# Later releases for the second and third weights load in the start-up of a linear-attention and MLP kernel

## The chip, the cores and the metric

The kernel runs on one core of a Trainium2 chip. The metric is the time of one execution on the device, in microseconds (us). An execution's span, as the profiler records it, is a little shorter than that time.

## The reference

Two blocks follow one another. The first is a linear attention with a decaying state (RWKV6): 4 batches, 8 heads, 768 tokens, 48 channels per head. The second takes its output as rows of 384 numbers and applies a small MLP with 2048 hidden channels, whose activation is h - tanh(h).

```python
for t in range(S):
    kt, vt, rt, wt = (k[:, :, t], v[:, :, t], r[:, :, t], w[:, :, t])
    cur = np.einsum('bhd,bhe->bhde', u[None] * kt, vt)
    y[:, :, t] = np.einsum('bhd,bhde->bhe', rt, state + cur)
    state = wt[:, :, :, None] * state + np.einsum('bhd,bhe->bhde', kt, vt)
...
h = x @ w_in
g = h - np.tanh(h)
return (g @ w_out).astype(np.float32)
```

All is float32 to the outside, and the weights are passed as they are (no arithmetic on the host).

## The kernel before, in words

The 3072 tokens are worked off in eight blocks of 384 tokens (4 batches times 2 halves of the sequence). Inside a block, the attention is computed in six chunks of 64 tokens, for four pairs of heads. For each block the result is laid down transposed, as three tiles `xT0` to `xT2` (xT in the profile) of 128 channels by 384 tokens, which feed the MLP. The MLP takes 16 steps f per block: `first` (L883) multiplies xT by one tile of `w_in` and gives h, ScalarE and VectorE form g, and `Second.add` (L962) or other products add g times `w_out`. While the MLP of one block runs, the attention of the next is prepared between its steps. The instructions of TensorE (PE), VectorE (DVE), ScalarE (ACT) and SyncE (SP) run in the order in which the program lists them: each engine has one queue, and an instruction that waits holds up all behind it on that engine. SyncE's instructions are the starts of transfers.

The first block has no MLP to hide behind. Its attention is computed in `boot` (from L1140), in two halves of two head pairs each, called h1 and h2. The order there is written out by hand. For each half:

- `behind`, `before`, `times_behind`, `times_before` form running products of the decay on VectorE;
- `own` and `earlier` compute the scores (L494): `own` those of a token with itself (the diagonal mask), `earlier` those with the tokens before it in its chunk, the off-diagonal ones;
- `turn_1` (L517) and `turn_2` (L523) transpose the keys;
- `update_half` (L616) makes, with 24 small matmuls on TensorE, what each chunk adds to the state;
- `states_half` (L631) carries the state from chunk to chunk on VectorE;
- `result` multiplies scores with v (L698) and states with the decayed r (L679), and `result_out` (L741) copies the outcome out of PSUM into xT, on ScalarE and VectorE.

Head pairs 0 to 2 go to their own xT tile; each tile has holes of 16 rows, which pair 3, kept in the tile `late`, fills by six copies of 24 KB from on-chip memory to on-chip memory (`fill_holes`, L789), three begun by SyncE and three by GpSimd.

The weights arrive as raw tiles (`raw`, 768 KB each) by transfers that SyncE begins (`load_weights`, L251, called by `more_weights`). Sixteen loads bring all weights, and five buffers hold the raw tiles. The first and second load bring the first four steps' tiles of `w_in`; the third brings the first two steps' tiles of `w_out`; the fourth brings `w_in` again. Each raw tile is then converted (`convert`): three steps on ScalarE (L264), of which one writes `w_sb` and two write `up`, and a joining step on VectorE (L268). In `boot`, `first_a`, `second_a`, `third_a` are the ScalarE steps for the first three loads, and `first_b`, `second_b`, `third_b` the VectorE steps. In ScalarE's order `second_a` comes before the last `result_out` of the block, and `third_a` after it.

When a load of weights may start is fixed by `begin_behind(ins, load)`: the load waits until the instruction `ins` is done. Before the change, the second load follows the last matmul of the first half's `update_half`, the third the last matmul of the second half's `own` scores, and the fourth the last matmul of the second half's `earlier` scores (`scored`). The first load waits for nothing, and behind the fourth come the next block's `w` and more weights.

Of the kernel before, what the change touches and what calls it, by code (L numbers as in the profile page):

```python
# [50 lines left out]
B, H, S, D = 4, 8, 768, 48  # L51
# [4 lines left out]
NCH = NB // L  # L56
# [70 lines left out]
def kernel(  # L127
# [12 lines left out]
    nc = tc.nc  # L140
# [29 lines left out]
    start = const.tile([P, UP * NCH * LP], F32, name="start", tag="start")  # L170
# [77 lines left out]
    def load_weights(n, queue):  # L248
        raw = conv.tile([P, 2 * DM, 2], I32, name="raw", tag="raw")
        src = weights[UNITS[n]].bitcast(I32).rearrange("p (n two) -> p n two", two=2)  # L250
        return *UNITS[n], raw, queue.dma_start(out=raw, in_=src)  # L251

    def convert(part, j, raw, _, tiles=1):

        lo, hi = raw[:, :, 0], raw[:, :, 1]
        a = w_sb[:, part, 2 * j:2 * j + 2].rearrange("p f c -> p (f c)").bitcast(I32)
        up = conv.tile([P, 2 * DM], I32, name="up", tag="up", bufs=4)
        low, high = (up.bitcast(t).rearrange("p (n two) -> p n two", two=2)[:, :, i]  # L260
                     for i, t in enumerate((U16, F16)))

        def scaled(to, of, scale, bias=0.0):
            return lambda: nc.scalar.activation(out=to, in_=of, func=AF.Copy, scale=scale, bias=bias)  # L264

        return [scaled(a.bitcast(F32), hi.bitcast(F32), HIGH_SCALE), scaled(high, hi.bitcast(F32), SIGN_SCALE),
                scaled(low, lo.bitcast(U32), *LOW)], [
                lambda of=slice(i * 2 * DM // tiles, (i + 1) * 2 * DM // tiles): nc.vector.scalar_tensor_tensor(  # L268
                    out=a[:, of], in0=a[:, of], scalar=3, in1=up[:, of], op0=ALU.logical_shift_left,
                    op1=ALU.bitwise_or) for i in range(tiles)]  # L270
# [43 lines left out]
    def begin_behind(ins, then):  # L314
        tc.add_manual_dep(then.ins, ins.ins.name, mybir.DependencyInfo(
            mybir.DependencyClass.Sync, mybir.DependencyReason.DATA))
# [3 lines left out]
    class Block:  # L320
# [186 lines left out]
        def own(self, ps, p0, **fill):  # L507
            return self.masked(ps, "k", "r", masks["diagonal"], p0, **fill)

        def earlier(self, ps, p0, **fill):  # L510
            return self.masked(ps, "post", "pre", masks["above"], p0, **fill)
# [90 lines left out]
        def update_half(self, pair, p0):  # L602

            self.by_column = [t[:, 0:D * NCH].rearrange("d (e c) -> d e c", c=NCH) for t in pair]
            for x in range(UP):
                if x:
                    nc.tensor.drain().then_inc(fence, 1)
                    fences.append(None)
                    nc.tensor.wait_ge(fence, len(fences))
                for c in range(0, NCH, 2):  # L610
                    for h in range(2):
                        for par in range(2):
                            p = (x + par) % UP
                            toks = slice(64 * par, 64 * par + 64)
                            e0 = (p0 + p) * D2 + h * D
                            self.done = nc.tensor.matmul(self.by_column[p][64 * h:64 * h + 64, :, (c + par + 1) % NCH],  # L616
                                             lhsT=self.ks[toks, p0 + p, c // 2, 64 * h:64 * h + 64],
                                             rhs=self.v[toks, c // 2, e0:e0 + D], start=True, stop=True)

        def totals_by_column(self, p0):  # L620

# [259 lines left out]
    def first(xT, f, hp, apart=0):  # L881
        for kc in reversed(range(KC)):
            nc.tensor.matmul(hp, lhsT=w_in_sb[:, f, kc, :], rhs=xT[kc],  # L883
                             start=(kc == KC - 1), stop=(kc == 0))
            for _ in range(apart):
                nc.tensor.nop(nofuse=True, hint="apart")
        h = dense.tile([P, NB], F32, name="h", tag="h")
        return h, nc.scalar.activation(out=h, in_=hp, func=AF.Copy, scale=1.0 / UPSCALE)  # L888
# [228 lines left out]
    def more_weights(queue):  # L1117
        raws.append(load_weights(more_weights.n, queue))
        more_weights.n += 1
        return raws[-1][-1]  # L1120
# [3 lines left out]
    def run(ops):  # L1124
        for op in ops:
            op()
# [13 lines left out]
    def boot(ps, pair, blk, later):  # L1140
        h1, h2 = HALVES
        blk.tiles["w"] = states0
        for name, p0, n in (("w", h1 + 1, 1), ("w", h1, 1), ("k", h1, UP), ("r", h1, UP), ("w", h2, UP)):
            blk.load(name, p0, n)
        blk.load_v()
        blk.load("k", h2, UP)
        blk.load("r", h2, UP)
        more_weights(nc.sync)

        both = (h1, h1 + 1), (h2, h2 + 1)  # L1150
        blk.behind(h1 + 1, 1)
        blk.behind(h1, 1)
        blk.take_whole(h1, UP)
        blk.totals_by_column(h1)
        nc.scalar.copy(out=later_ident, in_=ident)
        blk.before(h1, UP)
        blk.times_behind(h1, UP)
        blk.times_u(h1, UP)
        own = blk.own(ps, h1, spare=94, ahead=5, late=6)
        blk.turn_1(ps, h1)  # L1160
        blk.times_before(h1, UP)
        earlier = blk.earlier(ps, h1)
        blk.behind(h2, UP)
        blk.take_whole(h2, UP)
        first_a, first_b = convert(*raws.pop(0), tiles=2)
        own()
        blk.turn_2(h1)
        blk.totals_by_column(h2)
        blk.update_half(pair, h1)
        begin_behind(blk.done, more_weights(nc.sync))  # L1170
        blk.times_behind(h2, UP)
        blk.times_u(h2, UP)
        blk.turn_1(ps, h2)
        blk.turn_2(h2)
        earlier()
        blk.results(ps)
        blk.result("from_scores", both[0])
        blk.in_turn(both[0])
        run(blk.states_half(h1))
        blk.result("from_states", both[0], True, apart=True)  # L1180
        blk.before(h2, UP)
        blk.update_half(pair, h2)
        blk.times_before(h2, UP)
        own = blk.own(ps, h2)
        own_scored = blk.done
        run(first_a[:1])
        blk.result_out((3,), [nc.scalar.copy] * 2)
        blk.result_out((2,))
        earlier = blk.earlier(ps, h2, ahead=1)
        scored = blk.done  # L1190
        onwards = blk.states_half(h2)
        own()
        run(first_a[1:])
        needed = 2 * KC - 2
        blk.fill_holes([nc.sync, nc.gpsimd], range(needed, 2 * KC))
        begin_behind(own_scored, more_weights(nc.sync))
        blk.fill_holes([nc.sync, nc.gpsimd], range(needed))
        begin_behind(scored, more_weights(nc.sync))
        later.load("w")
        second_a, second_b = convert(*raws.pop(0))  # L1200
        third_a, third_b = convert(*raws.pop(0))
        run(second_a)
        more_weights(nc.sync)
        blk.results(ps)
        blk.yp.reverse()
        blk.result("from_states", both[1], apart=True)
        blk.in_turn(both[1])
        earlier(1, 1)
        earlier(0, 1)
        for p in reversed(both[1]):  # L1210
            blk.result("from_scores", (p,), True)
        later.load("k")
        more_weights(nc.sync)
        run(onwards)
        run(first_b[:1])
        for p in reversed(both[1]):
            blk.result_out((p,), [nc.scalar.copy, nc.vector.tensor_copy])
        run(first_b[1:])
        run(third_a[:2])
        run(second_b)  # L1220
        blk.held(0, NPAIR)
        return [(third_a[2], third_b)]
# [6 lines left out]
    with tc.tile_pool(name="ps_boot", bufs=1, space=PSUM) as ps_boot:  # L1229
        pieces = boot(Turns([scratch(ps_boot)] + ps_a.both), [hp] + acc, blocks[0], blocks[1])  # L1230
# [30 lines left out]
    for i, blk in enumerate(blocks):  # L1261
# [9 lines left out]
        for f in range(NF):  # L1271
# [5 lines left out]
            h, made = first(here, f, to[:, 0:NB], SPACED[i][f > 12 + (i < 2)])  # L1277
# [190 lines left out]
```

## Time and profile before

| what | value |
|---|---|
| time, median of 3 runs | 544.36 us |
| lowest and highest | 544.14 and 544.81 us |
| the profiled execution's own time | 543.88 us |
| its span | 542.2 us |
| TensorE busy | 534.0 us (98%) |
| VectorE busy | 459.3 us (85%) |
| ScalarE busy | 404.2 us (75%) |
| transferred | 56.34 MB, of which the 16 weights loads are 768 KB each |

All times in a profile are counted from the start of the span. A timeline row gives start, duration, engine, line, operation, tile written and tiles read, and how many instructions were merged; in brackets stand the time that the engine was idle before it, and what ended that wait. SPq and POOLq are the instructions by which SyncE and GpSimd begin a transfer. PEld is TensorE's loading of weights into its array, which overlaps with its matmuls.

### The profile page before, as it was taken

The page shows a single profiled execution, that of the slowest core. Times are in us where ns is not written, and L with a number is a line of the kernel's source. Part 1 is how long each engine was busy: PE and PEld are TensorE (multiplying, and loading weights), DVE is VectorE, ACT ScalarE, POOL GpSimd, SP SyncE. Part 2 cuts the span into 40 slices and gives each one's busy share as a digit, 9 for nine tenths or more (in the row PEclk, how much of TensorE's full clock was granted, in tenths as well). Part 3 has the DMA queues.
Part 4 walks back from the last instruction along what each step waited for, and adds up shares of the span by engine and source line. Part 5 has one row for each costly group of instructions (what it writes and reads, how often), then busy time and mean ns, then how long its engine had stood idle before and what let it go on. Part 6 is the DMA issues. An engine that isn't in the chain of part 4 may idle for free.

```text
span 542.2 us, 14874 instructions
## 1 busy us (share of the span) xinstructions
PE 534.0 (98%) x5682; PEld 403.4 (74%) x5682; DVE 459.3 (85%) x943; ACT 404.2 (75%) x814; POOL 7.0 (1%) x51
## 2 busy tenths in 40 slices
PE   8999999999999999999999999999999999999996
PEld 5756665678787777877887787877788788777874
DVE  7999999999989989798997989879797997557563
ACT  4999996897668886688767886688766885766561
POOL 1100000000000000000000000000000000000000
PEclk9999999999999999999999999999999999999999
DMA  7799642342311642154122622135321510100101
GB/s 276 242 403 348 219 119 71 122 112 81 106 48 46 162 118 57 44 148 119 61 56 87 132 92 70 50 102 145 90 84 45 118 31 3 56 1 0 45 1 47
DMA packets 53048, 56.34 MB, mean 104 GB/s; under 512 B 21488, under 2 KB 50928, under 8 KB 52976
## 3 DMA queue, kind: packets, MB, share of 16 engines
q1 hardware_dynamic: 52592, 55.18, 33.5%
q8 instruction: 48, 0.79, 0.6%
q14 instruction: 24, 0.20, 0.1%
q10 hardware_dynamic: 288, 0.10, 0.1%
q0 software_dynamic: 96, 0.07, 0.1%
HBM read 44.73 MB, written 4.72 MB: 91 GB/s over the span
## 4 chain that ended last, share of the span: by engine, by line
PE 95%; DVE 2%; DMA 1%; issue 0%; PEld 0%; SPq 0%; PEldq 0%; DVEq 0%
PE hp L883 44%; PE acc L1011 27%; PE att L1011 7%; PE acc L962 5%; PE att L769 4%; PE att L494 2%; PE acc L989 2%; PE att L575 1%; PE att L883 1%; DMA r<-in_rT 1%; PE acc L883 1%; DVE scores L502 1%; DVE post L429 0%; PE att L989 0%; PEld att L679 0%
## 5 line engine op out<-in xcount | busy, mean ns | idle before, releaser
L883 PE MATMUL hp<-xT,w_sb 128*128 128x384 f32 x738 | 259.2, 487 | 0.5 <-DVE w_sb L268 0.5
L883 PEld LDWEIGHTS hp<-xT,w_sb 128*128 128x128 f32 x738 | 131.9, 190 | 69.7 <-issue 0.6
L1011 PE MATMUL acc<-forms,g 128*128 128x128 f32 x954 | 133.2, 276 | 0.0
L888 ACT ACTIVATE h<-hp 128x384 f32<-128x384 f32 x123 | 60.4, 491 | 97.2 <-PE hp L883 97.1
L1011 PEld LDWEIGHTS acc<-forms,g 128*128 128x128 f32 x954 | 122.0, 192 | 10.3
L891 DVE SCALAR_TENSOR_TENSOR h<-h,s 128x384 f32<-128x384 f32 x128 | 70.6, 552 | 51.6 <-ACT s L906 51.5
L932 DVE TENSOR_TENSOR g<-g 128x256 f32<-128x256 f32 x265 | 103.4, 420 | 7.3 <-PE acc L1011 6.5
L907 ACT ACTIVATE qa<-s,shift 128x384 f32<-128x384 f32 x113 | 69.5, 615 | 3.7
L909 ACT ACTIVATE junk<-s,shift 128x384 bf16<-128x384 f32 x113 | 67.7, 599 | 0.0
L891 DVE SCALAR_TENSOR_TENSOR g<-qa,h 128x384 f32<-128x384 f32 x112 | 61.7, 551 | 1.6 <-ACT qa L917 0.2
L906 ACT ACTIVATE s<-h 128x384 f32<-128x384 f32 x113 | 59.1, 523 | 3.5
L1011 PEld LDWEIGHTS acc<-w_sb,g 128*128 128x128 f32 x318 | 46.7, 191 | 9.7 <-ACT sums L979 0.3
L1011 PE MATMUL acc<-w_sb,g 128*128 128x128 f32 x318 | 53.0, 276 | 0.0
L1011 PE MATMUL att<-w_sb,g 128*128 128x128 f32 x212 | 35.5, 275 | 0.0
L1011 PEld LDWEIGHTS att<-w_sb,g 128*128 128x128 f32 x212 | 31.1, 192 | 5.3
L1046 DVE TENSOR_TENSOR sums<-sums 128x256 f32<-128x256 f32 x84 | 32.9, 407 | 1.7 <-ACT sums L1023 1.4
L962 PE MATMUL acc<-w_sb,sums 128*128 128x384 f32 x96 | 33.7, 487 | 0.0
L264 ACT ACTIVATE up<-raw 128x768 f16<-128x768 f32 (+1 forms) x32 | 33.1, 1074 | 0.0
L962 PEld LDWEIGHTS acc<-w_sb,sums 128*128 128x128 f32 x96 | 18.0, 190 | 12.3 <-DVE sums L891 0.3
L417 DVE TENSOR_TENSOR_SCAN pre<-w,start 128x780 f32<-128x780 f32 x14 | 25.0, 1783 | 0.8
L429 DVE TENSOR_TENSOR_SCAN post<-w,seed 128x780 f32<-128x780 f32 x14 | 24.9, 1776 | 0.0
L909 ACT ACTIVATION_READ_ACCUMULATOR junk<-s,shift 128x1 f32 x113 | 21.1, 186 | 0.0
(119 smaller groups left out, 530.5 us busy)
## 6 DMA issues: line engine op xcount, KB each, us to landing
raw<-in_weights SPq DMA_DIRECT2D x16, 768.0 KB, 7.0
w<-in_wT SPq DMA_DIRECT2D x7, 780.0 KB, 4.5
k<-in_kT SPq DMA_DIRECT2D x7, 768.0 KB, 4.6
r<-in_rT SPq DMA_DIRECT2D x7, 768.0 KB, 4.5
v_sb<-in_v SPq DMA_DIRECT2D x8, 576.0 KB, 3.9
k<-in_tokens SPq DMA_DIRECT2D x7, 576.0 KB, 5.0
r<-in_tokens SPq DMA_DIRECT2D x7, 576.0 KB, 4.8
out_y<-sums SPq DMA_DIRECT2D x18, 128.0 KB, 1.8
```

The lines of the kernel that those rows point to most:

```text
L264: return lambda: nc.scalar.activation(out=to, in_=of, func=AF.Copy, scale=scale, bias=bias)
L417: return nc.vector.tensor_tensor_scan(out=self.tile("pre")[:, cols], data0=self.tile("w")[:, cols], data1=start[:, 0:n * NCH * LP], initia ...
L883: nc.tensor.matmul(hp, lhsT=w_in_sb[:, f, kc, :], rhs=xT[kc], start=(kc == KC - 1), stop=(kc == 0))
L888: return h, nc.scalar.activation(out=h, in_=hp, func=AF.Copy, scale=1.0 / UPSCALE)
L891: return lambda: nc.vector.scalar_tensor_tensor(out=out, in0=in0, scalar=scalar, in1=in1, op0=op0, op1=ALU.mult)
L906: nc.scalar.activation(out=s, in_=h, func=AF.Square)
L907: nc.scalar.activation(out=qa, in_=s, func=AF.Square, bias=shift[:, 4:5])
L909: nc.scalar.activation(out=junk[:, 0:NB], in_=s, func=AF.Relu, bias=shift[:, 5:6], accum_out=excess[:, at:at + 1])
L932: return lambda: nc.vector.tensor_tensor(out=G[:, to:to + 2], in0=two(G, g_at(q, a0), g_at(q, a1)), in1=two(G, g_at(q, b0), g_at(q, b1)), ...
L962: nc.tensor.matmul(acc, lhsT=g[:, j * P:(j + 1) * P], rhs=w_out_sb[:, f, :], start=(f == self.first), stop=(f == NF - 1))
L1011: nc.tensor.matmul(to, lhsT=G[:, g_at(q, a), :], rhs=rhs, start=start, stop=stop, skip_group_check=True)
L1046: ops.append(lambda op=op, at=at: nc.vector.tensor_tensor(out=at[0], in0=at[1], in1=at[2], op=OPS[op]))
```

## The change

`update_half` now returns its first matmul. The second load of raw weights waits for the first matmul of the second half's `update_half`, not for the last one of the first half's. The third load waits for `scored`, the last off-diagonal score of the second half, not for the last diagonal score, and SyncE begins it after all its copies of `fill_holes`, where it stood between the first and the other two. The fourth load is released by `scored` as before.

```diff
         def update_half(self, pair, p0):
...
+            first = None
...
-                            self.done = nc.tensor.matmul(self.by_column[p][64 * h:64 * h + 64, :, (c + par + 1) % NCH],
-                                             lhsT=self.ks[toks, p0 + p, c // 2, 64 * h:64 * h + 64],
-                                             rhs=self.v[toks, c // 2, e0:e0 + D], start=True, stop=True)
+                            made = nc.tensor.matmul(self.by_column[p][64 * h:64 * h + 64, :, (c + par + 1) % NCH],
+                                                    lhsT=self.ks[toks, p0 + p, c // 2, 64 * h:64 * h + 64],
+                                                    rhs=self.v[toks, c // 2, e0:e0 + D], start=True, stop=True)
+                            first = first or made
+            return first
...
         blk.update_half(pair, h1)
-        begin_behind(blk.done, more_weights(nc.sync))
         blk.times_behind(h2, UP)
...
-        blk.update_half(pair, h2)
+        begin_behind(blk.update_half(pair, h2), more_weights(nc.sync))
         blk.times_before(h2, UP)
         own = blk.own(ps, h2)
-        own_scored = blk.done
...
         blk.fill_holes([nc.sync, nc.gpsimd], range(needed, 2 * KC))
-        begin_behind(own_scored, more_weights(nc.sync))
         blk.fill_holes([nc.sync, nc.gpsimd], range(needed))
+        begin_behind(scored, more_weights(nc.sync))
         begin_behind(scored, more_weights(nc.sync))
```

## The prediction

> **What bounds the kernel now.** I read the page first, then the sums over long windows, then the timelines of the first 30 us engine by engine, and last the transfers' times from issue to landing.
>
> ```profile
> span 542.2 us, 14874 instructions
> PE 534.0 (98%) x5682; PEld 403.4 (74%) x5682; DVE 459.3 (85%) x943; ACT 404.2 (75%) x814; POOL 7.0 (1%) x51
> L883 PE MATMUL hp<-xT,w_sb 128*128 128x384 f32 x738 | 259.2, 487 | 0.5 <-DVE w_sb L268 0.5
> ```
>
> TensorE is busy for 534.0 of 542.2 us, so nearly all the time is matmuls that this change leaves alone. In the first layer's largest group it idled 0.5 us in all, waiting for VectorE to put a weight tile together. The next view gives busy time by engine (PE, PEld, DVE, ACT, POOL) in two windows.
>
> ```profile
> 29.00:51.00 22.00, 22.00 (x135) 13.46 (x137) 21.28 (x38) 21.90 (x31) 0.00 (x0) 1.00 1.01 391
> 53.00:540.00 487.00, 484.36 (x4920) 370.49 (x4918) 411.90 (x860) 359.15 (x751) 2.37 (x27) 1.00 0.29 81
> ```
>
> From 29 to 51 us, while weights are still being converted, VectorE (21.28 of 22.00) and ScalarE (21.90) are full beside TensorE. After 53 us only TensorE is (484.36 of 487). So a delay that VectorE or ScalarE has at 29 us cannot be caught up by 51 us, and whatever reaches TensorE at 52 us stays to the end. The 0.5 us wait of the page is exactly there:
>
> ```profile
> 52.04 2.17 PE L883 MATMUL hp<-xT,w_sb 128*128 128x384 f32 x6 [0.46 <-DVE w_sb L268]
> ```
>
> The question is therefore what the moved loads do to ScalarE and VectorE before 29 us. The timelines there, starts and durations in us, of TensorE:
>
> ```profile
> 13.14 0.22 PE L616 MATMUL hp<-v_sb,ks 64*64 64x48 f32 x1
> 16.39 0.25 PE L616 MATMUL acc<-v_sb,ks 64*64 64x48 f32 x1
> 19.93 0.22 PE L494 MATMUL att<-pre,post 48*64 48x64 f32 x1
> ```
>
> These are the last update matmul of the first half, the first one of the second half and the last off-diagonal score: the old release of the second load, its new one, and the new release of the third. The issuing queues, SyncE's and GpSimd's:
>
> ```profile
> 13.44 0.34 SPq L251 DMA_DIRECT2D raw<-in_weights  x1
> 17.70 0.64 SPq L789 DMA_DIRECT2D xT<-late  x1
> 18.52 0.43 SPq L251 DMA_DIRECT2D raw<-in_weights  x1
> 19.00 1.15 SPq L789 DMA_DIRECT2D xT<-late  x2
> 20.25 0.53 SPq L251 DMA_DIRECT2D raw<-in_weights  x1
> 16.97 1.58 POOL L789 DMA_DIRECT2D xT<-late  x3 [1.53 <-ACT late L741]
> ```
>
> The three rows of raw are the second, third and fourth load. The second leaves at 13.44, 0.08 us after its matmul ends (13.14 + 0.22). The six small copies that fill the holes of xT stand around the third load. And ScalarE:
>
> ```profile
> 19.44 0.92 ACT L264 ACTIVATE w_sb<-raw 128x768 f32<-128x768 f32 x1
> 20.23 2.02 ACT L264 ACTIVATE up<-raw 128x768 f16<-128x768 f32 x2
> 22.83 0.96 ACT L741 COPY xT<-att 48x384 f32<-48x384 f32 x2 [0.58 <-PE att L698]
> 23.83 0.91 ACT L264 ACTIVATE w_sb<-raw 128x768 f32<-128x768 f32 x1
> 24.63 1.06 ACT L264 ACTIVATE up<-raw 128x768 f16<-128x768 f32 x1
> 25.87 0.49 ACT L888 ACTIVATE h<-acc 128x384 f32<-128x384 f32 x1 [0.17 <-PE acc L883]
> ```
>
> The three steps at 19.44 and 20.23 read the second load. Behind them, in the same queue, stand the copies that finish xT, then the third load's conversion, then the first h. The only idle times are 0.58 and 0.17 us.
>
> **The change, part by part.** No arithmetic is added or removed. Transfers start later and change places on SyncE. How long they take, from five issues of the same 768 KB weights load (asked for at 13.44, 18.52, 50.51, 54.84 and 58.64; last column is us from issue to landing):
>
> ```profile
> raw<-in_weights SPq DMA_DIRECT2D x1, 768.0 KB, 4.3
> raw<-in_weights SPq DMA_DIRECT2D x1, 768.0 KB, 5.3
> raw<-in_weights SPq DMA_DIRECT2D x1, 768.0 KB, 4.2
> raw<-in_weights SPq DMA_DIRECT2D x1, 768.0 KB, 4.1
> raw<-in_weights SPq DMA_DIRECT2D x1, 768.0 KB, 4.5
> ```
>
> *The second load.* Today it lands at 13.44 + 4.3 = 17.74, 1.7 us before ScalarE reads it at 19.44. Its new release ends at 16.39 + 0.25 = 16.64; with the same 0.08 us it is issued at 16.72, 3.28 us later. That exceeds the cover of 1.7 us, so ScalarE must wait. For how long hangs on the transfer. Nothing shows it at 16.72, so it is bounded by 4.1 us (alone) and 5.3 us (the load at 18.52, which shares its time with the hole copies). The new slot lies beside GpSimd's three copies, issued from 16.97, and ahead of SyncE's, so neither row is plainly nearer; I take 4.8 us, between the undisturbed 4.3 and the 5.3. It lands at 21.52. The three conversion steps take from 19.44 to 20.23 + 2.02 = 22.25, that is 2.81 us, and so end at 24.33; with the 0.04 us that usually lie between steps the xT copies start at 24.37 instead of 22.83. The 0.58 us that ScalarE idled there is used up: they are 1.54 us late.
>
> The Trainium skill (DMA: Bandwidth & Descriptors, section "Anatomy of one DMA") fits a DMA of the software path at 2.0 us and its bytes at 436 GB/s; for 786,432 bytes that is an estimate of 3.8 us, and by it the load would land at 20.52 and the end move by 0.4 us, which could not be measured. All five rows here are above it, at 4.1 to 5.3 us, so the rows decide.
>
> *What waits behind it.* VectorE makes the other halves of these copies, and TensorE's weight loads for the first h wait for those and for the holes:
>
> ```profile
> 23.34 1.05 DVE L741 COPY xT<-att 48x384 f32<-48x384 f32 x2 [0.28 <-ACT xT L741]
> 23.18 0.30 PEld L883 LDWEIGHTS acc<-xT,w_sb 128*128 128x128 f32 x2
> 24.11 0.30 PEld L883 LDWEIGHTS acc<-xT,w_sb 128*128 128x128 f32 x2 [0.63 <-DVE xT L741]
> 24.92 0.30 PEld L883 LDWEIGHTS acc<-xT,w_sb 128*128 128x128 f32 x2 [0.51 <-DVE xT L741]
> ```
>
> *The hole copies.* Here the change gives something. SyncE's copy of 17.70, ahead of the third load, and its two of 19.00 and about 19.6, behind it, landed after
>
> ```profile
> xT<-late SPq DMA_DIRECT2D x1, 24.0 KB, 2.0
> xT<-late SPq DMA_DIRECT2D x1, 24.0 KB, 5.0
> xT<-late SPq DMA_DIRECT2D x1, 24.0 KB, 5.2
> ```
>
> so at 24.0 and 24.8, while VectorE's two copies were done by 23.34 + 1.05 = 24.39. The weight load at 24.92 really waited for the last hole, not for VectorE. With the third load behind them these two leave at about 18.3 and 18.9, behind only the second load, and land near 21.5: no wait is left on them. Without them the last weight load could go about 0.32 us earlier (0.65 us of matmuls after one at 23.95). But the xT copies are 1.54 us late, so it goes at 24.60 + 1.54 = 26.14, 1.2 us later than now, and its result comes 0.9 us after that, near 27.05.
>
> *The third and fourth loads.* The last off-diagonal score ends at 20.15, SyncE is free by then, and the third load leaves at about 20.25, 1.73 us later; the fourth, now with the same release, 0.5 us later. At 4.3 to 5.3 us the third lands at 24.55 to 25.55. ScalarE, late anyway, wants it at 23.83 + 1.54 = 25.37: covered within 0.2 us. If ScalarE were on time, this load would be the next to be late, by 0.7 to 1.7 us.
>
> *The sum.* ScalarE's third conversion starts at 25.37, its next step at 26.17 ends at 27.23, and the first h at 27.25 instead of 25.87: 1.38 us, the 1.54 less the 0.17 us of idle time there. VectorE is tied to this:
>
> ```profile
> 26.39 0.56 DVE L914 CUSTOM_DVE_ANT_0 s<-h 128x384 f32<-128x384 f32 x1 [0.46 <-ACT h L888]
> 27.35 0.96 DVE L268 SCALAR_TENSOR_TENSOR w_sb<-w_sb,up 128x768 int32<-128x768 int32 x1 [0.40 <-ACT up L264]
> 28.99 0.56 DVE L891 SCALAR_TENSOR_TENSOR sums<-qa,h 128x384 f32<-128x384 f32 x1 [0.21 <-ACT qa L917]
> 50.96 1.80 DVE L268 SCALAR_TENSOR_TENSOR w_sb<-w_sb,up 128x768 int32<-128x768 int32 x2
> ```
>
> All its idle time before 29 us ends with ScalarE; from 28.99 to the tile that TensorE awaits at 52.04 it has none to give back. So 1.38 us arrive at 52.04, and stay: span 543.6, profiled execution 543.88 + 1.38 = 545.3. The median of the three runs, 544.36, lies 0.48 above that execution; on it the forecast is 545.7.
>
> **The rivals.** *A short transfer.* Everything happens as above, but the load takes 4.1 to 4.3 us, as three of the five rows did. The end moves by 0.7 to 0.9 us: about 545.2. For it: most rows; against it: the hole copies beside it.
>
> *A late chain.* Not only the second load but also the stream behind the third is late, and later conversions wait again. The sixth load, issued at 22.38, landed 12.5 us later, at 34.88, and ScalarE took it at once:
>
> ```profile
> raw<-in_weights SPq DMA_DIRECT2D x1, 768.0 KB, 12.5
> 34.91 0.91 ACT L264 ACTIVATE w_sb<-raw 128x768 f32<-128x768 f32 x1
> ```
>
> Pushed back by the third load's full 1.73 us it lands at 36.61, and ScalarE wants it at 34.91 + 1.38 = 36.29: 0.3 us more, and with a second load of 5.3 us (another 0.5) about 546.5. Against it: the stream no longer has the holes in it and may run faster.
>
> *Not slower: the holes decide.* If the second load landed by 19.98 (22.83 less 0.04 less 2.81), ScalarE's 0.58 us would hide it, and the earlier holes would be what is left: h at about 25.72, 0.15 us sooner, 544.2. It needs a transfer within 3.26 us; no row is below 4.1.
>
> **How the numbers follow.** A measurement of this kernel can tell about 0.2% (1.09 us) from no change; the forecast passes that if the transfer takes over about 4.5 us. Chances: forecast 0.55, short transfer 0.24, late chain 0.09, holes decide 0.08, and 0.04 for a gain that no row shows. Slower by over 0.2%: 0.55 + 0.09 = 0.64; within: 0.24 + 0.08 = 0.32; faster 0.04. The bounds of the transfer alone, 4.1 to 5.3 us, give 545.0 to 546.3; the range reaches to 544.7 and 546.6 to take in half of what lies outside. Cases of slower hold most of the chance.
>
> **What would show it.** In the changed kernel's profile: the second load issued near 16.7 and landing near 21.5; ScalarE idle for about 2 us before the conversion step now at 19.44, its releaser the DMA; no 0.58 us idle before the xT copies; the first h near 27.2; VectorE's step now at 50.96 and TensorE's at 52.04 later by the same amount, about 1.4 us, and nothing lost after. The forecast is wrong if that load lands before 20, if ScalarE's delay is gone by 51 us, or if the page shows new idle time of TensorE after 53 us.

## The result and the profile after

The changed kernel takes 549.5 us (median of six runs, 548.51 to 550.57), the kernel before, run beside it, 544.25 us (six runs, 543.87 to 544.81). The ratio is 1.0096 with a 95% interval of 1.0084 to 1.0108: slower by 1.0%, or 5.25 us. The prediction said slower by 1.38 us, with a range up to 546.6. The direction was right and the size was not. The profiled execution took 548.51 us, 4.63 more than the one of before; it is the fastest of the six.

The head of the page after, and the same group of matmuls as before:

```profile
span 546.8 us, 14873 instructions
PE 535.4 (98%) x5682; PEld 404.3 (74%) x5682; DVE 459.3 (84%) x943; ACT 403.7 (74%) x814; POOL 6.9 (1%) x51
L886 PE MATMUL hp<-xT,w_sb 128*128 128x384 f32 x738 | 259.2, 487 | 0.3 <-DVE w_sb L268 0.3
```

The work is the same; TensorE is busy for 1.4 us more (535.4 against 534.0) and idle for the rest of the 4.6 us. (Below `update_half`, line numbers are 3 higher in the changed kernel: L883 is now L886, L888 is L891, L741 is L744.) Now the start-up, first SyncE's queue and the load's time to landing:

```profile
17.34 0.34 SPq L251 DMA_DIRECT2D raw<-in_weights  x1
18.18 2.04 SPq L792 DMA_DIRECT2D xT<-late  x3
20.59 0.81 SPq L251 DMA_DIRECT2D raw<-in_weights  x2
```
```profile
raw<-in_weights SPq DMA_DIRECT2D x1, 768.0 KB, 6.5
```

The second load leaves at 17.34 and lands 6.5 us later, at 23.88. The trace has 16 completion events for each such load. Fifteen of this one came by 21.80, 4.5 us after the issue, and only the last at 23.88. ScalarE, in the timeline:

```profile
23.90 0.89 ACT L264 ACTIVATE w_sb<-raw 128x768 f32<-128x768 f32 x1 [3.84 <-DMA raw<-in_weights]
24.69 1.95 ACT L264 ACTIVATE up<-raw 128x768 f16<-128x768 f32 x2
26.51 0.81 ACT L744 COPY xT<-att 48x384 f32<-48x384 f32 x2
29.31 0.49 ACT L891 ACTIVATE h<-acc 128x384 f32<-128x384 f32 x1 [0.24 <-PE acc L886]
...
32.83 0.49 ACT L891 ACTIVATE h<-acc 128x384 f32<-128x384 f32 x1 [1.33 <-PE acc L886]
```

It waits 3.84 us for the load, the first h starts at 29.31 instead of 25.87 (3.44 us late), and the second h later still: 32.83, where the kernel before had

```profile
27.97 0.49 ACT L888 ACTIVATE h<-acc 128x384 f32<-128x384 f32 x1
```

so 4.86 us late. The bracket of the second row names its cause, a wait for TensorE. TensorE's clock shows why (columns: window and its length; busy time of PE, PEld, DVE, ACT, POOL; granted clock; share of the DMA engines; GB/s):

```profile
25.50:28.92 3.42, 1.31 (x4) 0.86 (x5) 1.90 (x4) 3.42 (x6) 0.00 (x0) 1.00 1.03 392
28.92:32.33 3.41, 3.41 (x7) 1.72 (x6) 2.65 (x6) 2.35 (x4) 0.00 (x0) 0.50 1.05 393
32.33:53.00 20.67, 20.67 (x74) 12.67 (x73) 18.59 (x34) 20.17 (x29) 0.00 (x0) 1.00 0.91 333
58.00:545.00 487.00, 484.22 (x4920) 370.43 (x4918) 411.79 (x860) 358.62 (x750) 2.35 (x27) 1.00 0.29 81
```

TensorE, without xT, is busy for only 1.31 of the 3.42 us to 28.92; for the next 3.41 us it is granted half its clock, just when it makes the first two h. From 32.33 on it is full again. The hand-over that was at 50.96 and 52.04 comes at

```profile
55.83 1.80 DVE L268 SCALAR_TENSOR_TENSOR w_sb<-w_sb,up 128x768 int32<-128x768 int32 x2
```
```profile
56.91 2.17 PE L886 MATMUL hp<-xT,w_sb 128*128 128x384 f32 x6 [0.30 <-DVE w_sb L268]
```

both 4.87 us late, as the second h was, and the span is 4.6 us longer. After that nothing is lost: TensorE is busy for 484.22 us in the 487 us from 58, against 484.36 in the 487 us from 53 before.

So there are two losses in this execution where the prediction had one: the second load takes 6.5 us, not 4.8, and TensorE's wait is followed by one window at half its clock.

### The profile page after: what moved, and what is told of

Read it like the earlier page. It is cut to its first block, busy times and chain, and to the rows that moved or that the text cites. A ratio compares the mean times of both kernels' runs of the same rounds, so it can differ in the third digit from the quotient of the medians.

```text
span 546.8 us, 14873 instructions
## 1 busy us (share of the span) xinstructions
PE 535.4 (98%) x5682; PEld 404.3 (74%) x5682; DVE 459.3 (84%) x943; ACT 403.7 (74%) x814; POOL 6.9 (1%) x51
## 4 chain that ended last, share of the span: by engine, by line
PE 91%; DVE 3%; ACT 3%; DMA 2%; issue 1%; SPq 0%; PEldq 0%; PEld 0%; DVEq 0%
PE hp L886 43%; PE acc L1014 26%; PE att L1014 6%; PE acc L965 4%; PE att L772 4%; PE att L494 2%; PE acc L992 2%; ACT up L264 1%; PE att L575 1%; DMA raw<-in_weights 1%; PE acc L886 1%; DMA r<-in_rT 1%; DVE post L443 1%; DVE pre L417 0%; DVE w_sb L268 0%
## 5 line engine op out<-in xcount | busy, mean ns | idle before, releaser
L886 PE MATMUL hp<-xT,w_sb 128*128 128x384 f32 x738 | 259.2, 487 | 0.3 <-DVE w_sb L268 0.3
L886 PEld LDWEIGHTS hp<-xT,w_sb 128*128 128x128 f32 x738 | 132.0, 191 | 69.7 <-issue 0.4
L891 ACT ACTIVATE h<-hp 128x384 f32<-128x384 f32 x123 | 60.3, 490 | 97.5 <-PE hp L886 97.4
```

## The experiments

Fourteen runs were made, thirteen of other kernels and one of the changed kernel again, each beside the kernel before on the same chip. Diffs marked "to before" or "to after" are against that kernel. Letters in the quoted expectations are those of the theories when each was written; the text here names them in words.

**The second load's release alone** (to before, with `update_half` returning its first matmul):

```diff
         blk.update_half(pair, h1)
-        begin_behind(blk.done, more_weights(nc.sync))
...
-        blk.update_half(pair, h2)
+        begin_behind(blk.update_half(pair, h2), more_weights(nc.sync))
```

> Only the second load is moved; the third and fourth stay as before the change. Theory A (the loss is the second load's lateness: ScalarE's wait, and the half clock that TensorE is given after its idle time): about the whole loss, 548 to 551 us, with ScalarE waiting 2.5 to 4 us for the load and one stretch of 3.4 us at half clock. Theory B (the third load, late and behind the hole copies, holds a part of 1 us or more): clearly less than the whole, below 548 us.

**The third load's release and place alone** (to before):

```diff
-        begin_behind(own_scored, more_weights(nc.sync))
         blk.fill_holes([nc.sync, nc.gpsimd], range(needed))
         begin_behind(scored, more_weights(nc.sync))
+        begin_behind(scored, more_weights(nc.sync))
```

> Only the third load is moved (released by the last off-diagonal score, after all hole copies); the second stays as before. Theory A: ScalarE is then on time and wants the third load at 23.8 us, while it lands between 24.6 and 25.6: 0.7 to 1.7 us later on ScalarE, 545.0 to 546.0. Theory B: at least as much, with more waits at the fifth and sixth load: over 546. Holes landing earlier can give 0.15 us back at most.

The first took 548.25 us (547.17 to 550.39; ratio 1.0080, 1.0058 to 1.0102), the second 545.4 us (544.24 to 547.7; 1.0020, 1.0008 to 1.0032). ScalarE in the first, then in the second:

```profile
23.32 0.90 ACT L264 ACTIVATE w_sb<-raw 128x768 f32<-128x768 f32 x1 [3.23 <-DMA raw<-in_weights]
```
```profile
25.22 0.93 ACT L264 ACTIVATE w_sb<-raw 128x768 f32<-128x768 f32 x1 [0.88 <-DMA raw<-in_weights]
```

Most of the loss is the second load's; in this first run's profile TensorE had half its clock too, from 26.97 to 30.38 us. The third load, moved alone, makes ScalarE wait 0.88 us, inside the 0.7 to 1.7 us that the prediction gave for a ScalarE that is on time; with the second load late as well, that wait is hidden. In this second profile the second load, in its old place, took 5.6 us (15 of its completion events came by 17.74, the last at 19.08), without harm inside its cover. So the new place is not all that makes a load long.

**Half clock taken away** (to after; `busy` adds eight matmuls whose result nobody reads, while TensorE waits for xT):

```diff
         run(onwards)
+        busy(pair[1], 8)
         run(first_b[:1])
```

> The changed kernel with eight matmuls of 128x512 on the identity (about 0.4 us each, results unused) on TensorE between the last scores and the first matmul of the MLP, so that it isn't idle while it waits for xT. If the half clock is a cost of its own (1.7 us: 3.4 us at half speed), the time falls by 1 to 1.7 us against the changed kernel, to about 548, and the granted clock is 1.0 throughout. If the clock only costs time in which TensorE would have waited for ScalarE anyway, the time stays at 549 to 550.

It took 546.14 us (545.73 to 549.67; 1.0049, 1.0026 to 1.0072), below the 548 that was expected. In its profile the load took 5.5 us, and the window that was at half clock is

```profile
28.92:32.33 3.41, 3.41 (x12) 1.98 (x11) 2.79 (x6) 3.41 (x6) 0.00 (x0) 1.00 1.03 390
```

at full clock; its two h start at 28.04 and 30.14, 2.1 us apart as before (25.87 and 27.97), not 3.5. The runs form two groups: six at 545.73 to 546.3 us, with a mean clock of 0.998 or 0.999, and two at 549.65 and 549.67, with 0.993 and 0.995. Half clock is a loss of its own, 1.4 us between the two h of the changed kernel. What remains without it is the late load, here 1.7 us (546.14 less 544.46 of before beside it) with a transfer that was 1.0 us shorter than in the changed kernel's profile.

**The second load released between the two places** (to before: by the last matmul of the first half's scores times v):

```diff
         blk.update_half(pair, h1)
-        begin_behind(blk.done, more_weights(nc.sync))
...
         blk.result("from_scores", both[0])
+        begin_behind(blk.done, more_weights(nc.sync))
```

> The kernel before with the second load released by the last matmul of the first half's scores times v, which ends near 15.2 us: half way between 13.4 and 16.7. If a transfer at this place takes 4.3 us it lands at 19.6, inside ScalarE's 0.6 us of slack: 544.3, no loss. If a load here takes over 6 us, as the changed kernel's did, it lands near 21.7 and costs about 1.6 us without a change of clock: 546.

545.64 us (544.79 to 546.57; 1.0020, 1.0010 to 1.0031). The load, issued at 15.29, took 4.4 us, and ScalarE did not wait for it. Yet the kernel is slower, through something the prediction does not have:

```profile
21.53 0.50 PE L494 MATMUL att<-pre,post 48*64 48x64 f32 x18 [1.88 <-issue]
```

TensorE stops for 1.88 us in the middle of its scores, and the releaser is "issue": nothing that the profile shows. From 22.37 to 25.79 us, behind this stop, TensorE has half its clock. The changed kernel was then run and profiled **a second time, unchanged**, beside three of the kernels below:

> The changed kernel once more, beside the variants below: 548 to 551 us, with the second load landing 5.5 to 6.5 us after its issue, and one or two stretches of 3.4 us at half clock (mean granted clock 0.993 to 0.997). A load of 4.3 to 4.8 us here would say that the first profile caught a rare one.

549.69 us (547.33 to 550.15; 1.0077, 1.0055 to 1.0099). This time the load was issued at 16.78 and took 6.4 us, and the same stop is there, longer: 4.0 us in the waits, 4.18 us before this weight load. TensorE's clock is halved for two windows, from 20.83 to 27.66 us. The last off-diagonal score comes late through the stop, and so the third load, which it releases, leaves at 24.51 instead of 20.59.

```profile
PE att L494 <- issue: 4.0, 1, 4.0
```
```profile
23.57 0.61 PEld L494 LDWEIGHTS att<-pre,post 48*64 48x64 f32 x18 [4.18 <-issue]
```

What the stop is, the DMA view by windows suggests (queue, kind: packets, MB, share of 16 engines). Of the changed kernel's second profile, from 17 to 20.9 us and from 20.9 to 22.3 us:

```profile
q1 hardware_dynamic: 213, 0.84, 64.2%
q0 software_dynamic: 87, 0.07, 5.2%
```
```profile
q8 instruction: 1, 0.02, 5.4%
...
```

and of before, from 14.8 to 17.3 us, and from 17.3 to 18.3 us:

```profile
q1 hardware_dynamic: 130, 0.72, 74.3%
```
```profile
q0 software_dynamic: 13, 0.02, 8.8%
q8 instruction: 1, 0.02, 6.0%
...
```

q8 carries instructions, 16 KB in one packet. The trace's records of single packets and of completion events give the times (last column: when 15 of the load's 16 events were there, and the last):

```
kernel                   fetches of 16 KB begin at     data of the second load             events: 15, last
before                   13.8, 17.3, 22.7              14.4 to 17.4                        17.66, 17.70
changed, first profile   13.8, 17.6, 21.5              18.3 to 21.2 (120 of 128 rows)      21.80, 23.88
changed, second profile  13.8, 20.95, 24.7             17.8 to 20.96                       21.53, 23.21
released at 15.29        13.9, 19.35, 22.7             16.3 to 19.1                        19.66, 19.70
kept busy                14.0, 17.6, 22.0              18.2 to 21.6                        22.35, 22.67
third load alone         14.0, 17.6, 21.3              14.5 to 18.7                        17.74, 19.08
```

In the kernel before, the load just fits between two fetches. Its last row ends (17.35) when the fetch begins (17.34), so this fetch may have been held a little already, without a stop. Where the load meets the fetch that otherwise comes at 17.3, more than one thing is seen. In the changed kernel's first profile the fetch is first, and the load's last event comes 2.1 us after the other 15. In the second profile the load is first. The fetch starts only when the load's data are through, some 3.6 us later than in the kernel before; the load's last event comes after that fetch, which ends at 22.16; and TensorE stands still, as if it had run out of instructions, until 1.4 us after the fetch ends (1.2 us in the kernel released at 15.29). Neither is a rule: in the kept-busy kernel the fetch is first too, and no event is late; with the third load alone one event is late by 1.3 us, in the old place. The other experiments test the meeting.

**All six hole copies by SyncE** (to after), in case GpSimd's copies stretch the load:

```diff
-        blk.fill_holes([nc.sync, nc.gpsimd], range(needed, 2 * KC))
-        blk.fill_holes([nc.sync, nc.gpsimd], range(needed))
+        blk.fill_holes([nc.sync], range(needed, 2 * KC))
+        blk.fill_holes([nc.sync], range(needed))
```

> The changed kernel with all six hole copies begun by SyncE, behind the second load on its queue, none by GpSimd. Theory C (GpSimd's copies, which share the DMA engines with the second load, stretch it): the load takes 4.3 to 4.8 us and the time falls by 1 to 2 us. Theory D (what stretches it is one engine held by something else, as a fetch of instructions): the load still takes 5.5 to 6.5 us and the time is the changed kernel's, 548 to 551, or above it by the longer queue on SyncE.

547.8 us (546.73 to 548.29; 1.0059, 1.0043 to 1.0076). The load still took 6.4 us (issued at 16.88, a fetch at 17.6, 120 of its 128 rows done by 20.6, the last at 22.8), and ScalarE waited 3.73 us for it:

```profile
23.32 0.90 ACT L264 ACTIVATE w_sb<-raw 128x768 f32<-128x768 f32 x1 [3.73 <-DMA raw<-in_weights]
```

GpSimd's copies are not what stretches it. The time is below the 548 to 551 that was expected, and below the 549.69 of the changed kernel beside it: in this profile TensorE has neither the long stop nor half its clock.

**The third load behind all hole copies, released as before** (to before):

```diff
-        begin_behind(own_scored, more_weights(nc.sync))
         blk.fill_holes([nc.sync, nc.gpsimd], range(needed))
+        begin_behind(own_scored, more_weights(nc.sync))
```

> The kernel before with the third load moved behind all hole copies, but with its old release, the last diagonal score. The copies land near 21 instead of 24.8, and the third load leaves near 19.6 instead of 18.5 and is wanted at 23.8. If it takes 4.3 to 4.6 us as in the run with only the third moved, it lands at 23.9 to 24.2: between 0.15 us faster and 0.4 us slower than before, 544.2 to 544.8. If the order of the copies mattered more than my sum has it, faster by over 1 us.

545.45 us (544.4 to 547.0; 1.0020, 1.0009 to 1.0032), against an expectation of 544.2 to 544.8. The third load left at 19.92 instead of 18.52, and ScalarE waited 1.64 us for it. Whatever the earlier hole copies give is less than that costs.

**The second load 1 us earlier** (to before: behind the first matmul of the first half's updates):

```diff
-        blk.update_half(pair, h1)
-        begin_behind(blk.done, more_weights(nc.sync))
+        begin_behind(blk.update_half(pair, h1), more_weights(nc.sync))
```

> The kernel before with the second load released by the first instead of the last matmul of the first half's updates, about 1.0 us earlier (12.4). It is then over by about 16.7, before TensorE's fetch near 17.4. Theory E: 543.8 to 544.5, and fewer executions above 545. If only the load's lateness counts, no change: it is 1.7 us ahead already.

546.88 us (543.4 to 548.14; 1.0034, 1.0016 to 1.0051): the expectation failed, because it overlooked the fetch at 13.8. Issued at 12.58, the load took 5.9 us, and that fetch began only at 16.5, behind the load's data (done at 16.1). In the waits of TensorE:

```profile
PE att L494 <- issue: 1.3, 1, 1.3
PE att L682 <- issue: 1.1, 1, 1.1
```

The same stop thus comes at the other edge of the gap. The runs scatter: four of twelve lie at 543.4 to 545.4 us with a mean clock of 0.998 to 1.0, one at 546.76 with 0.999, and seven at 546.6 to 548.1 with 0.989 to 0.995.

**An extra load at the new place** (to before, shortened here: 768 KB that nobody reads, into the buffer of the fifth load, requested behind the first update matmul of the second half; the second load stays early):

```diff
         blk.update_half(pair, h2)
+        begin_behind(blk.first, nc.sync.dma_start(out=extra_raw[0], in_=...))
```

> The kernel before, with an additional load of 768 KB that nobody reads (into the fifth raw buffer, which the fifth load writes again later) at the release that the change gives the second load. ScalarE never waits for it. Theory E: the collision alone costs most of the loss: TensorE stops without a releaser or has half clocks in some executions, and the third load, behind it, is 1 to 2 us late: 546.5 to 550. Theory A (only the lateness of the second load and what follows from it): the third load is up to 1.5 us late and nothing else: 544.5 to 546.

547.82 us (545.75 to 549.47; 1.0065, 1.0044 to 1.0085). The extra load took 5.2 us, with a fetch just ahead of its data (17.4 and 18.0) and no late completion event; the second load's conversion did not wait. The third load and the hole copies came late instead; in TensorE's waits:

```profile
PE acc L886 <- DMA xT<-late: 1.7, 2, 1.3
```

So a load in this place costs 1.4 us and more even if nobody needs its data: by the lowest run 1.4, by the highest 5.1. This does not isolate the fetch, since the extra load also delays what stands behind it.

**The second load in four parts of 32 partitions**, in the changed kernel and, as a control, in the one before:

```diff
+        if n == 1:
+            parts = [queue.dma_start(out=raw[i * 32:i * 32 + 32], in_=src[i * 32:i * 32 + 32]) for i in range(4)]
+            return *UNITS[n], raw, parts[0]
```

> The changed kernel with the second load cut into four transfers of 32 partitions each, same release, same place; TensorE's instructions and their fetches are unchanged. Each piece puts two rows of 6144 bytes on an engine (about 0.5 us) where the whole put eight (1.9 us). Theory E (a fetch waits until an engine has worked off the transfer it is in): a fetch now waits 0.5 us at most, TensorE doesn't stop without a releaser, and the time falls from 549.6 to 546 to 547 (the load is still late, by some 1.5 us more for four issues). If the pieces are worked off as one, time and stop stay as in the changed kernel: 548 to 551.

> The same cut in the kernel before. It meets no fetch while it runs, and lands about 1.2 us later (four issues), inside the 1.7 us of cover: 544.0 to 544.6, no change; with fewer executions above 545 if some of those are fetches that met the load.

547.86 us (547.4 to 548.28; 1.0064, 1.0050 to 1.0079), above the 546 to 547 that was expected, and 545.14 us (544.19 to 546.48; 1.0016, 1.0005 to 1.0026). In the profile of the first, the parts were issued from 17.65 to 20.1, and a fetch at 17.9 came ahead of their data, so whether a fetch can pass between parts was not tested. TensorE did not stop and kept its full clock, and ScalarE waited 3.43 us: 3.5 us lost through the late load alone. The control was slightly slower, which had not been expected: its third load left at 19.05 instead of 18.52, and ScalarE waited 0.34 us for it; why it left later is not shown.

**The instruction pages moved.** `own(ps, h1, spare, ahead, late)` fixes how many matmuls without use keep TensorE awake at the start; another number of them moves all later borders between the 16 KB blocks of instructions, here called pages, and also shifts the start-up itself a little.

```diff
-        own = blk.own(ps, h1, spare=94, ahead=5, late=6)
+        own = blk.own(ps, h1, spare=136, ahead=5, late=3)
```

This, in the changed kernel and in the one before; and `spare=46, ahead=5, late=9` in the kernel that releases the load at 15.29:

> The changed kernel with 42 more of the tiny matmuls at the start and three fewer of the wide ones (about the same time, 78 instructions more), so that TensorE's 16 KB of instructions that came near 17.5 us are asked for about 1.1 us earlier, ahead of the second load. Theory E (the loss is the second load and TensorE's instruction fetch meeting on a DMA engine): no stop of TensorE without a releaser near 20 us, a load of 4.3 to 4.8 us, and a time some 1.4 us above the control with the same fetch. Theory F (a load at this place takes over 5.5 us for another reason): the load still takes 5.5 to 6.5 us and the time is 4 us or more above the control.

> The control: the kernel before with the same 42 more and three fewer matmuls at the start. All later fetches of instructions move too, so it may be off the kernel before by up to 1 or 2 us; if the fetch then meets the second load of 13.4 to 17.4 us, TensorE may stop here where it didn't.

> The kernel whose second load follows the first half's results, with 48 of the 94 tiny matmuls at the start left out and 3 more of the wide ones (about the same time, some 90 instructions fewer), so that TensorE's next 16 KB of instructions are asked for about 1 us later. If TensorE's stop of 1.9 us in the middle of the off-diagonal scores was a fetch of instructions held up by the weights load, the stop goes or moves, and the time is near 544.4. If it was anything else, the stop stays at the same matmul and the time at 545.6.

554.33 us (553.08 to 556.26; 1.0187, 1.0164 to 1.0209), 553.78 us (551.21 to 558.2; 1.0180, 1.0138 to 1.0223) and 549.33 us (548.97 to 549.63; 1.0086, 1.0071 to 1.0102). All three are disturbed in another place: after 60 us, where the kernel before has no such wait, TensorE's waits are, in the first two,

```profile
PE att L772 <- issue: 5.3, 3, 3.2
...
```
```profile
PE att L769 <- issue: 4.4, 3, 2.5
...
```

so this edit cost some 10 us by itself (9.59 in the control). With it, the change costs 0.55 us (554.33 less 553.78; the intervals overlap) instead of 5, and the load took 5.0 us. This fits the fetch, but it is no proof. The fetch near 17.5 hardly moved: it came at 17.3 in the changed kernel, still just ahead of the load's data at 18.4, and at 17.8 in the control, while some 1.1 us earlier was intended. And the control's start-up is late already: its second h starts at 29.79, against 27.97 in the kernel before and 29.97 in the changed kernel with the same pages. In the third kernel the load left late, at 16.55, and met the fetch again (data through at 20.3, fetch at 20.3); TensorE stopped twice, for 0.6 us each, and the expected 544.4 was far off.

## Why the prediction was right or wrong, point by point

*Carried to the end: right.* How late the second h starts (27.97 before) and how late the profiled execution ends (543.88 before), for every kernel that loses nothing later:

```
kernel                          second h   late by   execution   late by
control in four parts            28.88      0.91      544.79      0.91
third load alone                 29.04      1.07      544.86      0.98
third behind the hole copies     29.50      1.53      545.38      1.50
released at 15.29                29.90      1.93      545.69      1.81
extra load                       29.90      1.93      546.09      2.21
kept busy                        30.14      2.17      545.73      1.85
hole copies by SyncE             30.89      2.92      546.73      2.85
second load 1 us earlier         30.94      2.97      546.76      2.88
second load in four parts        31.41      3.44      547.40      3.52
second load alone                32.22      4.25      547.85      3.97
changed, first profile           32.83      4.86      548.51      4.63
changed, second profile          34.47      6.50      550.10      6.22
```

The two columns agree within 0.32 us. A delay at the start does stay to the end, as read from the full windows of VectorE and ScalarE.

*ScalarE must wait for the second load: right.* The releaser is the DMA in every kernel that releases the load at the new place.

*The transfer: the step that failed.* The prediction took 4.8 us between bounds of 4.1 and 5.3. At this place it took 6.5, 6.4, 6.4 (hole copies by SyncE), 5.9 (second load alone), 5.5 (kept busy) and 5.0 us (pages moved). In the changed kernel's two profiles 15 of the 16 completion events came 4.5 and 4.75 us after the issue, near the forecast; the last one came 2.1 and 1.7 us behind them. The bounds came from five issues elsewhere; the view that shows what else the engines carry at that time, the instruction queue in the DMA view, was not used. The issue, too, was at 17.34 and not 16.72 in the first profile, where all of the start-up was about 0.5 us later; in the second it was at 16.78. Together, 0.62 + 1.74 us: the load lands 2.36 us later than the forecast 21.52, and the first h, at 29.31 and not 27.25, is 2.06 us later.

The Trainium skill (DMA: Bandwidth & Descriptors, section "Anatomy of one DMA") fits a DMA of the software path at 2.0 us and its bytes at 436 GB/s, for this load an estimate of 3.8 us. The 5.0 to 6.5 us here are further from that than the rows before. The Trainium skill (DMA: Bandwidth & Descriptors, section "Queues, rings and completion order") says that an engine takes its queues in turn but drains a whole packet of several descriptors before it switches. The second profile fits that, with the fetch at 20.95 when the load's data were done at 20.96; which engine carried which packet, the records do not tell.

*"So 1.38 us arrive at 52.04": a step was missing.* Between the first and the second h the changed kernel loses another 1.42 us (4.86 less 3.44) to half clock; the prediction carries the first h's delay on unchanged and has no term for it. (Its "nothing lost after" is about the time after 52.04, and there it was right.) The Trainium skill (TensorE: Matmul & The Clock Gate, "Part 1: The HAM clock gate") gives a window of 3413 ns, which the 3.41 us agree with, and lets the clock fall after an idle window; here a window with 1.31 of 3.42 us busy was enough. Such a window does not always halve the clock: the hole copies by SyncE kept it full behind one with 1.48 of 3.41 us busy (25.10 to 28.51), the kernel released at 15.29 lost it behind 1.53 (18.96 to 22.37), and the second profile behind 1.99 (17.42 to 20.83). The idle time was in the prediction's own numbers: it held TensorE up without asking what the clock makes of that. In the second profile the half clock lies elsewhere, behind the stop: the first h is 6.53 us late (32.40) and the second no more than that.

*The third load: right where it could be seen,* by the run of that move alone. *The hole copies:* no gain that shows, but not in the way that was forecast. Landing "near 21.5" was right only where the second load stayed early (21.45 with the third load alone). In the changed kernel they landed from 22.91 to 24.73, behind the late load, and TensorE waited for one of them:

```profile
24.53 0.88 PE L886 MATMUL acc<-xT,w_sb 128*128 128x384 f32 x2 [0.81 <-DMA xT<-late]
```

That wait is hidden by the later one for xT (2.19 us, to 27.61). *The rival "late chain"* named the right sign of the error but another cause. In the first profile no conversion up to 34 us waits for a load again; in the second, ScalarE waits once more, for the third load:

```profile
30.67 0.90 ACT L264 ACTIVATE w_sb<-raw 128x768 f32<-128x768 f32 x1 [2.31 <-DMA raw<-in_weights]
```

The forecast had that load covered within 0.2 us; here it left 4 us late, behind the stop.

*What stays open.* Why the transfer is so long is not settled. Whose instructions q8 carries is not in the records; that they are TensorE's is argued from the stops, which end after the held fetch. Why the load's last event is 2.1 us late when the fetch goes first is not shown: the fetch packet itself takes 1 to 1.6 us. That the meeting is what makes the load long, rather than only coinciding with it, rests on the profiles' order of packets and on the moved pages, whose control was disturbed; the kept-busy kernel and the extra load, where a fetch also went first and no event was late, speak against its being the whole cause. Why one execution takes the one course and the next the other seems to be settled by tenths of a microsecond between issue (16.78 or 17.34) and fetch; only these two profiles speak for that, and the hole copies by SyncE speak against it (issue at 16.88, fetch first). The time that the other five executions of the result lie above the profiled one is explained only as far as the second profile resembles them.

By its median, no version was faster than the kernel before.

## What to carry to other kernels

Before a large load is moved in a start-up that is short of slack, look at what the DMA engines carry in its new slot, instruction fetches included: here a load that met one was often long itself, or the fetch came late and TensorE stopped. Price a late operand of TensorE twice, once for the wait and once for the clock that the wait can cost afterwards (here 1.4 us). A transfer's time in another slot says little of its time in a busier one, so the upper bound has to come from what it meets there.

## What was not expected of the hardware

A 16 KB instruction fetch began at 20.95 instead of 17.3, when the data of a 768 KB load were done at 20.96, and TensorE then stood for 4.0 us with "issue" as the only releaser. The Trainium skill (Runtime: NRT & Kernel Launch, section "Instruction fetch mechanics") has the same blocks of 16 KiB, fetched through a DMA queue of the sequencer's own, and calls the cost mostly hidden; in the kernel before no such stop shows, in these runs one does. Other numbers of unused matmuls at the start, which move the page borders and shift the start-up, cost the kernel before 1.8% (553.78 against 544.19 us beside it). And a window in which TensorE was 38% busy (1.31 of 3.42 us) was followed by one at half clock, while one at 43% (1.48 of 3.41 us) was not.
